# Four interleaved attention layers on one core: a plan that knows the blocks of PE's program, transfers that ScalarE may issue, a second score tile and another division in the last chunk

## The chip, the core and the metric

The kernel runs on one core of a Trainium2 chip. The metric is the time of one execution on the device in microseconds; of each kernel several runs are taken and their median is given. A profiled execution has a time of its own.

The engines are named as the profile names them: PE multiplies matrices (PEld is its loading of weights), DVE is the vector engine, ACT the scalar engine, POOL the general one, SP issues transfers.

## The reference

Four layers in the order A, B, A, B, each `x = x + attention(layernorm(x))`, on x of 2048 x 512 in float32, with 32 heads of 16. Cut to what matters:

```python
def _A_ref(x, wqkv, wo):                 # W, dil = 8, 2
    q, k, v = heads(x @ wqkv)
    idx = pos[:, None] - off[None, :]    # eight keys back, every second one
    logits = where(idx >= 0, einsum("bhsd,bhswd->bhsw", q, kg) * scale, -1e9)
    o = einsum("bhsw,bhswd->bhsd", softmax(logits), vg)
    return merge(o) @ wo

def _B_ref(x, wqkv, wo):                 # W = 256
    scores = q @ k.T * Dh ** -0.5        # the last 256 keys of each query
    p = softmax(where(mask, scores, -1e9))
    return merge(p @ v) @ wo
```

## The kernel before

**Tiling.** The sequence is cut into 8 chunks of 256 rows. Layers 0 and 1 run chunk by chunk (A of chunk c, then B of chunk c), then layers 2 and 3: sixteen pairs A0, B0 to A15, B15. Float32 products of activations and weights are made of three float16 products (high x high, high x low, low x high), which are PE's long part: `proj_t` (L1014) for queries and keys and `proj_n` (L1041) for values and the output.

**A chunk of layer A** (`layer_a`, L1117). Scores of 32 queries against a window of 39 keys are 64 small matmuls for each half of the chunk (L1172). ACT copies them out of the banks into one tile `s` (L1181), transfers put them in memory and fetch the eight wanted ones of each query back (`sd<-s`, `l<-sd`), DVE and ACT make the softmax, the result goes through memory once more (`ptd<-bands`, `ptt<-ptd`), and 128 small matmuls mix the values (L1281).

**A chunk of layer B** (`layer_b`, L1298). Queries and keys are split into high and low float16 parts (L1310, L1313), put in memory and fetched in another arrangement (`re<-eh`, `re<-el` L1323; `stk<-re` L1334). A first pass of scores (L1392) gives each query its maximum: DVE masks (L1411) and reduces (L1407), and the maximum goes through memory into two rows of the queries' tile (`md<-mt` L1443, `stk<-md` L1449). A second pass of scores (L1543) has the maximum subtracted already; ACT takes the exponential (L1553, L1565), POOL or DVE masks it (L1582, L1576), and PE multiplies by the values with a column of ones (L1598), so that row 16 of every 32 is the sum to divide by. ACT copies one half of the result (L1615), DVE adds the other (L1612). In all chunks but the last, transfers gather the sums (`rc<-os` L1661) and the rows (`oc<-os` L1666), a reciprocal is made of a small tile (L1670), spread again (`os<-scr`) and multiplied (L1684). In the last chunk the division is made in place per head (L1628 to L1631): transpose, reciprocal of 8 columns, transpose back, multiply; then the rows leave for `oc` (L1641, half of them issued by ACT). `finish` (L1063) splits `oc` into high and low (L1083, L1085), projects, adds x (L1093) and stores.

**What sets the order.** Nothing is scheduled by hand line by line. Every piece of work is a task of the class `Plan` (`add`, L515) with an engine, a cost, what it reads and writes, and the tiles that it holds. The table `ORDER` at the top gives each task a place in its engine's queue; a negative place sends the task to its other engine (`alt`). `Plan.order` (L542) then walks the queues with the costs and emits all instructions in one sequence, each engine's in the order of its places. The table was found outside the kernel, with these costs. For PE the planner also models a clock that halves when PE did little lately, and a store of instructions that is filled at a fixed rate (`FETCH`, `STORE`). All transfers but the four pairs of L1641 are SP's. `IDLE` filler tasks of three matmuls each (L1724) compute nothing that is read; they keep PE busy.

Of the kernel before, what the change touches and what calls it, by code (L numbers as in the profile page):

```python
# [18 lines left out]
P = 128  # L19
# [417 lines left out]
LAG = {"PE": 0.24, "DVE": 0.13, "ACT": 0.16, "POOL": 0.1, "SP": 0.0}  # L437
RATE = 0.33
SLOW = 0.25
LEAVE = {"Q": 0.13, "C": 0.185, "X": 0.15, "V": 0.17, "R": 0.13, "F": 0.105, "": 0.0}  # L440
AGAIN = {"PE": 0.0, "DVE": 0.11, "ACT": 0.12, "POOL": 0.055, "SP": 0.0}
RECENT, WARM, EDGE = 3.4, 0.31, 0.05
FETCH, STORE = 66.0, 130.0
SLACK = 0.6


class Buf:
# [1316 lines left out]
```

## Time and profile before

| | |
|---|---|
| three runs | 1448.49, 1453.19, 1457.79 us; median 1453.19 |
| profiled execution | 1448.63 us, span of its instructions 1446.9 us |
| mean granted clock of PE | 0.960 |
| busy: PE, DVE, ACT, POOL | 1315.5, 865.6, 827.1, 397.4 us |
| transfers | 195.20 MB at a mean of 135 GB/s |

The rows of the page and of its views read: line, engine, operation, what it writes and reads, the shape, how many; then busy time in us and the mean of one in ns; then the idle time of the engine just before them and who ended it. A row of waits reads: who waited, for whom, us in total, how many times, the longest. A row of the source view gives the shortest, the median and the longest duration in ns. Names ending in q are an engine's sequencer, which issues transfers. "Issue" as releaser means that nothing the profile shows was missing. A row of the windows gives for a stretch the busy time and count of PE, PEld, DVE, ACT and POOL, the granted clock, the share of the transfer engines and their rate.

### The profile page before, as it was taken

What the parts mean: (1) busy time and instruction counts of PE and PEld (TensorE: products, weight loads), DVE (VectorE), ACT (ScalarE), POOL (GpSimd) and SP (SyncE); (2) the same over time, 40 slices, a digit from 0 to 9 for tenths busy, and PEclk for the clock granted to TensorE, in tenths of its full rate; (3) what the DMA queues carried; (4) which work ended last, traced back from release to release, by engine and by line L of the source; (5) the groups of instructions that cost most, each with busy time, mean ns of one, the idle gap of its engine ahead of it and who ended that gap; (6) DMA issues with size and microseconds to landing.
All of it is one profiled execution on the core that took longest, in us unless ns stands there. A gap on an engine that the chain in (4) does not pass through costs nothing. (4 is left out here: it accounts for less than half of the span.)

```text
span 1446.9 us, 64325 instructions
## 1 busy us (share of the span) xinstructions
PE 1315.5 (91%) x28126; PEld 863.0 (60%) x28126; DVE 865.6 (60%) x1967; ACT 827.1 (57%) x1299; POOL 397.4 (27%) x848
## 2 busy tenths in 40 slices
PE   9998999899899989989889898999989898898987
PEld 7765566565575746657456464746657475564643
DVE  5636673753747567375662727566463746748495
ACT  7744666456554746636556473837557455564643
POOL 5131222213323122132133130413133321232441
PEclk9999999999999999999899999999999999999988
DMA  8874445535445364552635546364454635435322
GB/s 271 228 191 123 131 122 142 141 109 141 113 115 153 86 175 113 164 138 92 145 91 163 139 137 153 106 176 98 147 135 122 166 84 160 129 105 146 114 72 61
DMA packets 185234, 195.20 MB, mean 135 GB/s; under 512 B 92892, under 2 KB 123356, under 8 KB 184952
## 3 DMA queue, kind: packets, MB, share of 16 engines
q1 hardware_dynamic: 184696, 190.83, 48.6%
q8 instruction: 220, 3.60, 1.1%
q14 instruction: 62, 0.51, 0.1%
q10 hardware_dynamic: 256, 0.26, 0.1%
HBM read 94.11 MB, written 79.36 MB: 120 GB/s over the span
## 5 line engine op out<-in xcount | busy, mean ns | idle before, releaser
L1407 DVE TENSOR_REDUCE m<-banks 128x2 f32<-128x512 f32 x448 | 301.5, 688 | 8.7
L1553 ACT ACTIVATE p<-banks,sclB 128x896 f32<-128x896 f32 x224 | 220.8, 1007 | 69.6 <-PE banks L1543 65.0
L1411 DVE COPY_PREDICATED banks<-trm,banks 128x128 f32<-128x128 int16 x448 | 123.6, 291 | 147.2 <-PE banks L1392 131.6
L1582 POOL TENSOR_SCALAR_AFFINE_SELECT ps<-ps 64x256 f32<-64x256 f32 x300 | 119.5, 420 | 301.0 <-ACT ps L1565 294.2
L1582 POOL TENSOR_SCALAR_AFFINE_SELECT p<-p 64x256 f32<-64x256 f32 x292 | 116.4, 420 | 218.3 <-ACT p L1553 206.3
L1392 PE MATMUL banks<-stk,stk 48*64 48x128 f16 (+3 forms) x3584 | 140.5, 247 | 38.6 <-DMA stk<-re 12.0
L1392 PEld LDWEIGHTS <-stk 48*64 48x64 f16 x3584 | 81.5, 110 | 115.7 <-issue 89.1
L1543 PE MATMUL banks<-stk,stk 64*64 64x128 f16 (+3 forms) x3584 | 119.3, 240 | 23.4 <-DMA stk<-md 7.2
L1598 PE MATMUL banks<-p,v 64*32 64x192 f32 (+1 forms) x3584 | 122.0, 373 | 13.3 <-issue 8.5
L1565 ACT ACTIVATE ps<-banks,sclB 128x768 f32<-128x768 f32 x112 | 100.5, 901 | 40.6 <-PE banks L1543 33.0
L1543 PEld LDWEIGHTS <-stk 64*64 64x64 f16 x3584 | 70.1, 109 | 76.1 <-issue 61.6
L1313 DVE SCALAR_TENSOR_TENSOR el<-banks,eh 128x512 f16<-128x512 f32 x64 | 42.8, 688 | 101.4 <-ACT eh L1310 57.6
L1181 ACT COPY s<-banks 128x624 f32<-128x624 f32 x64 | 74.3, 1262 | 45.5 <-DMA sd<-s 19.0
L1598 PEld LDWEIGHTS banks<-p,v 64*32 64x32 f32 x3584 | 65.6, 110 | 48.3 <-issue 21.0
L1615 ACT COPY os<-banks 128x256 f32<-128x256 f32 x112 | 41.0, 372 | 85.0 <-PE banks L1598 83.5
L1598 PE MATMUL banks<-ps,v 64*32 64x64 f32 (+1 forms) x3584 | 71.8, 256 | 4.5 <-issue 4.3
L1598 PEld LDWEIGHTS banks<-ps,v 64*32 64x32 f32 x3584 | 66.3, 110 | 11.1 <-issue 8.1
L1026 PE MATMUL banks<-xh,wA0h 128*128 128x256 f16 x256 | 71.1, 278 | 1.4 <-DMA xh<-ht 1.1
L1281 PE MATMUL banks<-ptt,vs 39*32 39x64 f32 x4096 | 58.8, 239 | 14.3 <-DMA ptt<-ptd 7.7
L1027 PE MATMUL banks<-xl,wA0h 128*128 128x256 f16 x256 | 70.8, 276 | 0.4 <-DMA xl<-xn 0.4
L1612 DVE TENSOR_TENSOR os<-os,banks 128x256 f32<-128x256 f32 x104 | 42.1, 415 | 48.4 <-ACT os L1615 40.3
L1028 PE MATMUL banks<-xh,wA0l 128*128 128x256 f16 x256 | 70.9, 277 | 0.0
(217 smaller groups left out, 3070.5 us busy)
## 6 DMA issues: line engine op xcount, KB each, us to landing
stk<-re SPq DMA_DIRECT2D x256, 96.0 KB
sd<-s SPq DMA_DIRECT2D x128, 156.0 KB
re<-eh SPq DMA_DIRECT2D x128, 128.0 KB
ptt<-ptd SPq DMA_DIRECT2D x128, 96.0 KB
vs<-vd SPq DMA_DIRECT2D x64, 156.0 KB
vd<-ve SPq DMA_DIRECT2D x32, 256.0 KB
xm<-y SPq DMA_DIRECT2D x32, 256.0 KB
re<-el SPq DMA_DIRECT2D x64, 128.0 KB
```

The source lines that it names most:

```text
L1026: nc.tensor.matmul(ps[mp].t[:, i], wh, xh, start=k == 0, stop=False)
L1027: nc.tensor.matmul(ps[mp].t[:, i], wh, xl, start=False, stop=False)
L1028: nc.tensor.matmul(ps[mp].t[:, i], wl, xh, start=False, stop=k == 3)
L1181: nc.scalar.copy(S_.t.rearrange("p k (s r) -> p r s k", r=4)[:, 2 * i : 2 * i + 2], pbs[i].t[:, :, 0 : 8 * WIN].rearrange("p r (s k) -> p ...
L1392: nc.tensor.matmul(o, lhs, k, start=True, stop=True, tile_position=(64 * par, 64 * h))
L1407: nc.vector.tensor_reduce(out=m.t[:, :, u, qb], in_=ps.t[:, :, 0 : 2 * P], op=ALU.max, axis=AX.X)
L1411: nc.vector.copy_predicated(t[:, :, 0:64], trm[:, 0].bitcast(I16).unsqueeze(1).broadcast_to([P, 2, 64]), t[:, :, C : C + 64])
L1543: nc.tensor.matmul(ps.t[64 * h : 64 * h + 64, par, at + x0 : at + x0 + q1 - q0], stk[hf, kt][r, col, k0 : k0 + 64], stk[hf, 0][r, col, q0: ...
L1553: nc.scalar.activation(big.t[:, 2 * i : 2 * i + 2], ps.t[:, :, 0:448], AF.Exp, scale=scl["B", 1])
L1565: nc.scalar.activation(small.t.rearrange("p (i m) x -> p m i x", i=2), ps.t[:, :, 0:384].rearrange("p m (i x) -> p m i x", i=2), AF.Exp, s ...
L1582: E.affine_select(out=v, in_=v, pattern=[[0, 4], [a, 64]], compare_op=op, fill=0.0, base=0, channel_multiplier=-a)
L1598: nc.tensor.matmul(acc.t[32 * mm : 32 * mm + 32, h, q0:q1], vv[r, blk, 17 * hd : 17 * hd + 32], x.t[r, mm, x0 : x0 + q1 - q0], start=begin ...
```

## The change

- **Supply.** The store filled at a fixed rate is replaced by a count of PE's instructions: at place 140 of each block of 256 a block is asked for, and place 193 of the next block has to wait until 4.2 us after that. The number of instructions of each task (`rec`) is corrected with it, and so are some costs.
- **ScalarE may issue.** Ten kinds of transfers get `alt=("ACT", ...)`: `shelve`, `band`, `window`, `put`, `get` of layer A; `put`, `stack`, `mput`, `mget`, `gather`, `gather_o`, `spread` of layer B. In the program SP's issues go from 1656 to 1357 and ACT's from 8 to 307. The 60 transposing transfers stay on SP.
- **Two score tiles.** The pool of `s` has two buffers. The room comes from smaller constants: the value tiles share one padding, `maskt` is 256 wide, `nul` one column, `ones` and the padding's source use a buffer of the small exponentials, and the throw-away output of the norms is one byte wide. The first chunk's maxima write their masked scores back to the banks.
- **Last chunk.** After the addition PE spreads row 16 of every 32 over the 32 rows (four matmuls against a column of the identity), and DVE takes the reciprocal of all 256 columns and multiplies. The heads are taken in the order 0, 2, 1, 3 of their quarters, `oc` is split by halves of the features, not of the rows, and the output projection takes its first half of the features as soon as those are there.
- **Orders.** All tables are new, with 122 filler tasks in place of 110.

```diff
-IDLE = 110
+IDLE = 122
-LEAVE = {"Q": 0.13, "C": 0.185, "X": 0.15, "V": 0.17, "R": 0.13, "F": 0.105, "": 0.0}
+LEAVE = {"Q": 0.1, "C": 0.13, "X": 0.18, "V": 0.14, "R": 0.1, "F": 0.095, "": 0.0}
-FETCH, STORE = 66.0, 130.0
-SLACK = 0.6
+SLACK = 0.6, 0.25
+SUPPLY = 4.2
...
-                store = min(STORE, store + FETCH * (now - seen))
-                us = max(us / clock, (t.rec - store) / FETCH)
-                store = min(STORE, store + FETCH * us - t.rec)
-                seen = now + us
+                us /= clock
+                wait = 0.0
+                for x in range(n + 1, n + t.rec + 1):
+                    if x % 256 == 140:
+                        asked, told = told, now + wait + us * (x - n) / t.rec
+                    elif x % 256 == 193 and x > 256:
+                        wait = max(wait, asked + SUPPLY - now - us * (x - n) / t.rec)
+                n += t.rec
+                us += wait
...
-    for name, bufs in (("px", 4), ("pqm", 1), ("pk", 1), ("psc", 1), ...
+    for name, bufs in (("px", 4), ("pqm", 1), ("pk", 1), ("psc", 2), ...
...
+        halves = []
+        if last:
+            for g in range(2):
+                vh, vl = Val(oh), Val(ol)
+                halves.append([vh, vl])
+                sg = slice(2 * g, 2 * g + 2)
+                plan.add("ACT", 0.52, lambda sg=sg: nc.scalar.copy(oh.t[:, sg], o.t[:, sg]), r=vo[g], w=[vh])
+                plan.add("POOL", 1.12, lambda E, sg=sg: E.tensor_tensor(out=ol.t[:, sg], in0=o.t[:, sg], in1=oh.t[:, sg], op=ALU.subtract),
+                         r=[*vo[g], vh], w=[vl], mode="S", alt=("DVE", 0.6))
...
-            proj_n(T, 3, oh, ol, [vh, vl], t, ps, vps)
+            proj_n(T, 3, oh, ol, halves if last else [[vh, vl]] * 2, t, ps, vps)
...
-                    plan.add("SP", 0.64, put, r=ve[n], w=[vre[par][z]], size=128)
+                    plan.add("SP", 0.62, put, r=ve[n], w=[vre[par][z]], size=128, alt=("ACT", 0.68))
-                plan.add("SP", 1.3, stack, r=vre[0] + vre[1], w=[vst[hf, i, hp]], size=192)
+                plan.add("SP", 1.3, stack, r=vre[0] + vre[1], w=[vst[hf, i, hp]], size=192, alt=("ACT", 1.35))
...
-        for j in range(4):
+        for j in (0, 2, 1, 3) if final else range(4):
...
-                                    out=unread[:, x0 : 3 * P], in0=ps.t[:, par, x0 : 3 * P], in1=maskt[:, x0:], scale=1.0, scalar=NEG,
+                                    out=ps.t[:, par, x0 : 3 * P], in0=ps.t[:, par, x0 : 3 * P], in1=maskt[:, x0 - P :], scale=1.0, scalar=NEG,
...
-                def divide(hp=hp, hq=hq, hf=hf, acc=acc, sh=sh, f=both_):
-                    f()
-                    v = sh.t[:, 0:C].rearrange("p (b x) -> p b x", x=32)
-                    r = flat(os_[hf])[:, (2 * hp + hq) * C : (2 * hp + hq + 1) * C]
-                    a = acc.t[:, 0, 0:C]
-                    nc.vector.transpose(sh.t[:, 0:C], a)
-                    nc.vector.reciprocal(v[:, :, 16:17], v[:, :, 16:17])
-                    nc.vector.transpose(r.rearrange("p (b x) -> p b x", x=32), v[:, :, 16:17].broadcast_to([P, 8, 32]))
-                    nc.vector.tensor_mul(r, a, r)
-                plan.add("DVE", 2.0, divide, r=[vacc, vhf], w=[vos[hf][hp], vsh])
+                plan.add("DVE", 0.36, both_, r=[vacc, vhf], w=[vsm])
+                pb = Banks(psum, 1, [P, D])
+                def across(pb=pb, some=some):
+                    for m in range(4):
+                        nc.tensor.matmul(pb.t[32 * m : 32 * m + 32, 0:C], idf[:, 32 * m + 16 : 32 * m + 17].broadcast_to([P, 32]), some(),
+                                         start=True, stop=True, tile_position=(0, 32 * m))
+                def divide(pb=pb, sh=sh, some=some):
+                    nc.vector.reciprocal(sh.t[:, 0:C], pb.t[:, 0:C])
+                    nc.vector.tensor_mul(some(), some(), sh.t[:, 0:C])
+                plan.add("PE", 0.43, across, r=[vsm], w=[vpb], mode="C", act=0.107, rec=16)
+                plan.add("DVE", 0.75, divide, r=[vpb, vsm], w=[vos[hf][hp], vbr])
```

**Transfers of the last B chunk.** SP's queue before, where the rearranged queries and keys are fetched (`stk<-re`), the rows and sums of the chunk before leave (`oc<-os`, `rc<-os`), and the first maxima are put down (`md<-mt`):

```order
L1334 DMA stk_2_131<-re_7_1_25803 48x1x1024 x4
L1334 DMA stk_0_129<-re_7_0_25916 48x1x1024 x2
L1334 DMA stk_0_132<-re_7_0_25916 48x1x1024 x2
L1666 DMA oc_6_25739<-os_6_1_25961 16x1024 x4
L1661 DMA rc_6_25677<-os_6_1_25961 16x1x64 x4
L1334 DMA stk_2_134<-re_7_1_25803 48x1x1024 x2
L1443 DMA md_7_0_26279<-mt_7_0_26271 4x32x32 x2
```

ACT's queue in the changed kernel at the same place, between the last exponentials (`ps_6`) and copies (`os_6`) of the chunk before and the first of this one (`mt_7` is the maximum, `v` the values):

```order
L1589 ACTIVATE ps_6_6_26077<-banks,sclB_172 128x2x2x192
L1358 DMA stk_2_132<-re_7_1_25802 48x1x1024 x2
L1639 COPY os_6_1_25968<-banks 128x256 x2
L1358 DMA stk_0_130<-re_7_0_25917 48x1x1024 x2
L1358 DMA stk_0_127<-re_7_0_25917 48x1x1024 x2
L1694 DMA oc_6_25671<-os_6_1_25968 16x1024 x4
L1454 ACTIVATE mt_7_0_26266<-mr_7_0_26254 128x32
L1368 ACTIVATE v_134<-banks 128x32x16 x2
```

Ten issues that were SP's stand in ACT's queue, ahead of the first maximum of the chunk and of the copy of its values.

**Scores of layer A on PE.** The last A chunk before: one score task (32 matmuls of float32, `k` and `qm`) stands alone between maxima of layer B (`stk`) and projections; its fellow stands 17 rows above.

```order
L1392 LDWEIGHTS stk_0_129
L1392 MATMUL banks<-stk_1_130,stk_0_129 64x256
L1172 MATMUL banks<-k_7_22767,qm_7_23481 64x39 x32
L1046 LDWEIGHTS xl_7_23078
L1046 MATMUL banks<-wA2h,xl_7_23078 128x512
```

The same place in the changed kernel:

```order
L1057 LDWEIGHTS xl_7_23093
L1057 MATMUL banks<-wA2h,xl_7_23093 128x512
L1196 MATMUL banks<-k_7_23130,qm_7_23494 64x39 x64
L1416 LDWEIGHTS stk_0_127
L1416 MATMUL banks<-stk_2_129,stk_0_127 64x128
```

The two tasks follow each other. Such pairs are 17 of the 47 rows of this line before and 30 of 34 now.

**The last two heads on DVE.** Before, each head is added, transposed, inverted, transposed and multiplied in one go:

```order
L1612 TENSOR_TENSOR banks<-os_7_1_27072,banks 128x256
L1628 STREAM_TRANSPOSE sh_27248<-banks 128x256
L1629 RECIPROCAL sh_27248<-sh_27248 128x8
L1630 STREAM_TRANSPOSE os_7_1_27072<-sh_27248 128x256
L1631 TENSOR_TENSOR os_7_1_27072<-banks,os_7_1_27072 128x256
```

Now, for both heads:

```order
L1636 TENSOR_TENSOR os_7_1_27083<-os_7_1_27083,banks 128x256 x2
L1657 RECIPROCAL sh_27277<-banks 128x256
L1658 TENSOR_TENSOR os_7_1_27083<-os_7_1_27083,sh_27277 128x256
L1657 RECIPROCAL sh_27282<-banks 128x256
L1658 TENSOR_TENSOR os_7_1_27083<-os_7_1_27083,sh_27282 128x256
L1087 TENSOR_TENSOR ol_7_27303<-oc_7_26900,oh_7_27301 128x512
```

Both additions stand ahead of both reciprocals, and what follows is the split of one half of the features.

More of the change, by code (lines that the diff above doesn't have):

```diff
@@ L770 @@
     plan.begin("S")
+    plan.add("POOL", 0.3, lambda: nc.gpsimd.memset(ones.t[0:4, 0, 0:P], 1.0), w=[vone])
     plan.add("POOL", 1.8, lambda: nc.gpsimd.memset(ptt, 0.0), w=[vptt])
@@ L1054, in proj_n @@
                 nxt = Val(ps)
-                plan.add("PE", 0.217 if low else 0.433, lambda k=k, low=low: part(k, low), act=0.213 if low else 0.426,
-                         r=[*vals, vwt[T, s], *chain], w=[vps, nxt], mode="F")
+                plan.add("PE", 0.217 if low else 0.433, lambda k=k, low=low: part(k, low), act=0.213 if low else 0.426, rec=2 if low else 4,
+                         r=[*vals[k // 2], vwt[T, s], *chain], w=[vps, nxt], mode="F")
                 chain = [nxt]
@@ L1061, in rows, with finish @@
         return slice(c0 + t, c0 + C, 2) if T == "A" else slice(c0 + t * P, c0 + (t + 1) * P)
-    def finish(l, c, o, vo):
+    def finish(l, c, o, vo, last=False):
         T = layers[l]
@@ L1068, in finish @@
         oh, ol = (buf("poh", [P, 4, C], F16, "o", f"o{z}{l}_{c}") for z in "hl")
+        halves = []
[7 more added lines that the diff above has]
+                         r=[*vo[g], vh], w=[vl], mode="S", alt=("DVE", 0.6))
         for t in range(2):
             ps = Banks(psum, 1, [P, D])
-            vh, vl, vps = Val(oh), Val(ol), Val(ps)
+            vps = Val(ps)
+            if not last:
+                vh, vl = Val(oh), Val(ol)
             sl = slice(t * P, (t + 1) * P)
-            if T == "A":
+            if last:
+                pass
+            elif T == "A":
                 def part(x, sl=sl):
@@ L1247, in layer_a, with window, put, get @@
             vvs = Val(vs)
[L1249 removed]
+            def window(E, t=t, vs=vs):
                 x = vd[l][t]
                 for bb in range(2):
[L1252 removed]
+                    E.dma_start(vs.t[64 * bb : 64 * bb + WIN],
                                       bass.AP(tensor=x.tensor, offset=x.offset + (c * P + 64 * bb) * D, ap=[[D, WIN], [32 * D, 2], [1, D]]))
[L1255 removed]
+            def put(E, t=t):
                 x = ptd[t]
[L1257 removed]
+                E.dma_start(bass.AP(tensor=x.tensor, offset=x.offset, ap=[[130 * H, 64], [64 * H, WIN_], [1, 2 * H]]),
                                   bands[64 * t : 64 * t + 64].rearrange("p k s u -> p k (s u)"))
[L1260 removed]
+            def get(E, t=t):
                 x = ptd[t]
@@ L1350, in layer_b @@
         o = buf("po4", [P, 4, C], F32, "ob", f"oc{l}_{c}")
-        vog = []
+        vog = [[], []] if final else []
         os_ = {}
@@ L1394, in layer_b @@
                     if first:
-                        plan.add("PE", 0.172, scores, r=[vst[hf, 0, hp], vst[hf, now, hp]], w=[vps], mode="R", act=0.14, rec=8)
+                        plan.add("PE", 0.172, scores, r=[vst[hf, 0, hp], vst[hf, now, hp]], w=[vps], mode="R", act=0.14, rec=4)
                     else:
@@ L1448, in mget @@
                     p0 = 64 * par + 48
-                    nc.sync.dma_start(stk[hf, 0][p0 : p0 + 2, 4 * hp : 4 * hp + 4].rearrange("p u t -> p (u t)"), v[par])
+                    E.dma_start(stk[hf, 0][p0 : p0 + 2, 4 * hp : 4 * hp + 4].rearrange("p u t -> p (u t)"), v[par])
             plan.add("DVE", 0.13, mrow, r=vm, w=[vmr])
@@ L1514, in values @@
                                         o = o[:, qo * P : (qo + 1) * P]
-                                    nc.tensor.matmul(o, v[:, jj, 17 * h : 17 * h + 32], rhs, start=z == 0 and (b == 0 or first),
+                                    nc.tensor.matmul(o, v[:, 17 * (H * jj + h) : 17 * (H * jj + h) + 32], rhs, start=z == 0 and (b == 0 or first),
                                                      stop=z == 1 and b == 1, tile_position=(0, 32 * mm), skip_group_check=True)
                         nxt = Val(acc)
-                        plan.add("PE", 0.67, values, r=[vp2, *vvt[(c - 1 + b) % 3], *([chain] if chain else [])], w=[vacc, nxt], mode="C", act=0.16, rec=64)
+                        plan.add("PE", 0.67, values, r=[vp2, *vvt[(c - 1 + b) % 3], *([chain] if chain else [])], w=[vacc, nxt], mode="C", act=0.16, rec=32)
                         chain = nxt
@@ L1611, in both_ @@
                 def both_(acc=acc, some=some):
-                    nc.vector.tensor_tensor(out=acc.t[:, 0, 0:C] if final else some(), in0=some(), in1=acc.t[:, 1, 0:C], op=ALU.add)
+                    nc.vector.tensor_tensor(out=some(), in0=some(), in1=acc.t[:, 1, 0:C], op=ALU.add)
                 vhf = Val(os_[hf])
@@ L1673, in layer_b, with spread @@
         vbc = Val(os_[1])
-        def spread():
-            nc.sync.dma_start(flat(os_[1]), scr.t.unsqueeze(0).broadcast_to([16, 8, 4 * C]))
-        plan.add("SP", 0.55, spread, r=[vscr, *vog], w=[vbc], size=840)
+        def spread(E):
+            E.dma_start(flat(os_[1]), scr.t.unsqueeze(0).broadcast_to([16, 8, 4 * C]))
+        plan.add("SP", 0.55, spread, r=[vscr, *vog], w=[vbc], size=840, alt=("ACT", 0.65))
         vo = [[], []]
@@ L1697 @@
     for some in ((0,), (1, 2)):
-        pad = buf("ps1", [P, 2, 64], F32, "rc", f"pad{some[0]}")
+        pad = buf("pp7", [P, 4, 192], F32, "p7", f"pad{some[0]}")
         vpad = Val(pad)
@@ L1733 @@
             layer_b(l + 1, c)
-    both = {"DVE": nc.vector, "POOL": nc.gpsimd, "ACT": nc.scalar}
+    both = {"DVE": nc.vector, "POOL": nc.gpsimd, "ACT": nc.scalar, "SP": nc.sync}
     for t in plan.order():
```

112 lines of the change are left out of this document (53 added, 59 removed), and 789 rows, old and new, of the table ORDER.

## The prediction

> **What bounds the kernel now.** I read the page first, then what the tensor engine waited for, then the sync engine's issues line by line, and last the end of the span as a timeline.
>
> ```profile
> span 1446.9 us, 64325 instructions
> PE 1315.5 (91%) x28126; PEld 863.0 (60%) x28126; DVE 865.6 (60%) x1967; ACT 827.1 (57%) x1299; POOL 397.4 (27%) x848
> q8 instruction: 220, 3.60, 1.1%
> ```
>
> PE carries work for 1315.5 us and is idle for 1446.9 - 1315.5 = 131.4 us. No other engine is above 60%, so time can come out of this kernel in two ways only: PE waits less, or its busy time runs at a better rate. The third row is a queue that brings instructions: 3.60 MB in 220 packets is 16.4 KB each, and 2 x 28126 = 56252 PE instructions over 220 packets is 256 per packet. So PE's program arrives in blocks of 256. What the 131.4 us were spent on, by the longest rows of PE's own waits:
>
> ```profile
> PE banks L1598 <- issue: 12.8, 6, 4.2
> PE banks L1392 <- DMA stk<-re: 12.0, 14, 1.8
> PE banks L1392 <- DVE m L1407: 9.4, 25, 1.2
> PE banks L1281 <- DMA ptt<-ptd: 7.7, 12, 2.1
> PE banks L1543 <- DMA stk<-md: 7.2, 11, 1.6
> PE banks L1392 <- ACT s L1181: 5.5, 5, 2.9
> PE banks L1281 <- issue: 4.5, 7, 1.0
> PE banks L1543 <- DVE m L1407: 4.5, 13, 1.0
> PE banks L1048 <- ACT oh L1083: 4.4, 1, 4.4
> PE banks L1172 <- issue: 4.3, 5, 1.6
> PE banks L1543 <- issue: 3.5, 3, 1.5
> ```
>
> No single wait leads. "Issue" (nothing that the profile shows was missing) is 12.8 + 4.5 + 4.3 + 3.5 = 25.1 us, transfers 12.0 + 7.7 + 7.2 = 26.9 us, and VectorE and ScalarE share most of the rest. One of the issue stalls, in time:
>
> ```profile
> 644.41 0.85 PE L1598 MATMUL banks<-p,v 64*32 64x256 f32 x14
> 648.45 0.39 PE L1598 MATMUL banks<-p,v 64*32 64x192 f32 x7 [3.19 <-issue]
> ```
>
> It falls in the middle of one run of equal matmuls, whose data had all arrived. Counted along PE's records, sequencer records included, the long gaps of this kind stand at instruction 193 of a block of 256, wherever much fewer than 4.2 us lie between there and instruction 140 of the block before. That is the rule that the changed planner writes down, and the trace bears it out.
>
> **The change part by part.** The profiled execution took 1448.6 us around its span of 1446.9; the sum is made against 1448.6, which stands 4.6 us under the runs' median of 1453.2.
>
> *Supply of instructions.* The new planner charges each such place. I walked both orders with the mean interval that the trace gives each kind of matmul: before, 60 stretches from place 140 to place 193 hold less than 4.2 us of work, 50 us too little in all; in the new order 45 do, 35 us too little. That is 30% off 25.1 us. Nothing to 25.1 us gained; I take **-8**.
>
> *Transfers off the sync engine.* 299 of its 1656 issues move to ScalarE. Prices of an issue, and who was late for it:
>
> ```profile
> L1334 SPq DMA_DIRECT2D stk<-re x256: 536/588/1667, 113.4 to 1387.0; - x128
> L1661 SPq DMA_DIRECT2D rc<-os x120: 502/587/1581, 159.3 to 1383.1; - x120
> 1369.58 7.78 SPq L1334 DMA_DIRECT2D stk<-re x10
> DVE el L1313 <- DMA re<-eh: 27.5, 8, 5.9
> L1641 ACTq DMA_DIRECT2D oc<-os x8: 500/598/878, 1411.9 to 1431.6; - x8
> ```
>
> At 0.588 us each, 1656 issues fill about 970 of 1447 us, and in the last chunk ten follow each other for 7.78 us while PE and VectorE want what they bring. 299 x 0.588 = 176 us leave that queue, 18%. The gain lies between nothing (PE's wait is then the transfer's own flight, not its issue) and 26.9 us. 18% of 26.9 is 5; since the two lines that stand in such trains, stk<-re and re<-eh, give the most of what is moved, and VectorE's 27.5 us behind the same lines delays the maxima that PE waits for, I take twice that, **-10**. The Trainium skill (DMA: Bandwidth & Descriptors, Issuing engines are not separate DMA queues) says that starting transfers from several engines only saves the sequencer's issue time, usually small beside the transfer; here the trace has that issue time at two thirds of the span. By the page alone this term would be near nothing and the sum 10 us later.
>
> *What ScalarE pays.* 299 x 0.598 = 179 us of issuing come on top of its 827.1. Its idle time holds them by the sum (1006 of 1447). But what stands behind an issue that waits for its source stands still too: exponentials, copies out of the banks. PE's waits for ScalarE are 5.5 + 4.4 us in the two rows above; if they and their smaller kin, some 18 us without the score copies, grow as ScalarE's load (1006/827), that is 4; if everything that falls on a busy ScalarE (57% of 179 us) reached PE, 102. The nearest row says the small end; I take **+5**.
>
> *Second score tile.* L1181 copies scores into a tile that a transfer must first have emptied:
>
> ```profile
> ACT s L1181 <- DMA sd<-s: 19.0, 7, 5.2
> ```
>
> With two tiles this wait has no reason left, and the two score tasks of a chunk can follow each other on PE. Of it 5.5 us reached PE in the row above. Nothing to 5.5, if ScalarE is then late with something else or not: **-5**.
>
> *The last chunk.* Rows for the old division and the new one:
>
> ```profile
> L1628 DVE STREAM_TRANSPOSE sh<-banks 128x256 f32<-128x256 f32 x8 | 3.6, 450 | 0.3
> L1629 DVE RECIPROCAL sh<-sh 128x8 f32<-128x8 f32 x8 | 1.6, 206 | 0.3
> L1630 DVE STREAM_TRANSPOSE os<-sh 128x256 f32<-128x256 f32 x8 | 3.6, 446 | 0.3
> L1612 DVE TENSOR_TENSOR banks<-os,banks 128x256 f32<-128x256 f32 x8 | 3.4, 424 | 1.4 <-ACT os L1615 1.4
> L1631 DVE TENSOR_TENSOR os<-banks,os 128x256 f32<-128x256 f32 x8 | 3.4, 424 | 0.3
> L1230 DVE RECIPROCAL mx<-mx 128x64 f32<-128x64 f32 x16 | 8.8, 553 | 0.7
> ```
>
> Old, per head: 424 + 450 + 206 + 446 + 424 = 1950 ns. New: an addition, a reciprocal over 128x256 and a product, 424 + r + 424. From 8 to 64 elements the reciprocal grows by (553 - 206)/56 = 6.2 ns an element, so r = 206 + 248 x 6.2 = 1.74 us, an estimate, and the new chain is 2.59 us, 0.64 more for each of 8 heads; the planner counts 0.75 for r and product together. The Trainium skill (VectorE: DVE Perf Modes, First, the fixed hardware budget) has the reciprocal as an iterative divide repeated 8 times; by that and the page's 0.96 GHz r would be 2.1 us, an estimate, and the end 0.8 us later. The order puts both last additions ahead of both reciprocals, so the last product ends 0.42 + 2 x (1.74 + 0.42) = 4.7 us after the second addition begins, not 2.08 (1428.95 to 1431.03 below): +2.6. Against it stands what follows:
>
> ```profile
> 1428.95 0.42 DVE L1612 TENSOR_TENSOR banks<-os,banks 128x256 f32<-128x256 f32 x1
> 1430.61 0.42 DVE L1631 TENSOR_TENSOR os<-banks,os 128x256 f32<-128x256 f32 x1
> 1434.28 1.14 ACT L1083 CAST oh<-oc 128x512 f16<-128x512 f32 x2 [6.03 <-DMA oc<-os]
> 1434.96 0.61 PE L1048 MATMUL banks<-wB3h,oh 128*128 128x512 f16 x1 [4.44 <-ACT oh L1083]
> 1442.86 0.38 PE L1046 MATMUL banks<-wB3h,ol 128*128 128x512 f16 x1
> ```
>
> All 24 final projections wait for the last landing and take 8.3 us. In the new order half of them need only heads that were divided earlier, and fill the 3.3 us in which PE sat idle for that landing: up to -4.1. Together **-2**, between +3 and -5.
>
> *PE's added work.* 36 more filler matmuls and the 32 that carry the sums across. By the fillers' row, 48.3 us for 330, the 36 cost 5.3 if nothing hides them; they stand where PE would wait: **+2**, of 0 to 8.
>
> *Clock.* A stall can cost twice, where the granted clock falls with it:
>
> ```profile
> L1724 PE MATMUL banks<-idf 128*128 128x256 f16 x330 | 48.3, 289 | 5.1 <-ACT s L1181 1.7 <-POOL idf masks.py:199 1.4 <-DVE y L1093 0.9
> 200.00:250.00 50.00, 45.61 (x1138) 31.77 (x1135) 24.34 (x49) 33.97 (x53) 12.89 (x29) 1.00 0.44 124
> 250.00:300.00 50.00, 42.35 (x904) 24.50 (x904) 31.64 (x66) 19.82 (x31) 11.96 (x27) 0.83 0.55 138
> core 0: 1446.9 us, clock 0.960
> ```
>
> The stretch from 250 holds the longest stall and a clock of 0.83. A mean of 0.960 between full and half is 8% of the span, 116 us, at half, 58 us lost at most. The terms so far shorten PE's idle time by 18 of 131 us, 14%; the same share of 58, mostly on busy time, is 7: **-5**.
>
> The first chunk's maxima now write to the banks rather than to a throw-away tile; L1612 writes os in 415 ns and banks in 424, so 128 of them are some 1 us on an engine that is idle 40%: nothing, or 1 if it were full.
>
> Sum: -8 - 10 + 5 - 5 - 2 + 2 - 5 = -23. From the profiled run that is 1425.6, from the median 1430.2. I forecast the middle, **1428 us**, and 1408 to 1441 for this case alone.
>
> **Rivals.**
> *ScalarE becomes the gate (slower).* Place: the seams between chunks, as in the last one, where the new order has ten issues between the exponentials of one chunk and the first work of the next. Each waiting issue holds the engine, the exponentials behind it hold banks, and PE runs out of banks. 174 groups of issues move. The other terms give -28; for the result to lie above 1468, 1% over the median, ScalarE must cost about 47 us, so from 0.27 us of PE time per moved group it decides; at 0.3 it is 52 and the time is 1448.6 - 28 + 52 = 1473. For it: ScalarE already ends waits of every engine. Against: 43% of it is idle, and a group holds it for 0.6 to 2.4 us. Chance 0.16.
> *The waits only change names (no difference).* The distances along PE from projections to scores and from scores to exponentials are nearly what they were (11 us of PE work each, before and after), so a transfer that is hidden today stays hidden and one that is late stays late. Then supply (-8) is offset by ScalarE and fillers (+7), the rest moves to VectorE's maxima: 1446 to 1452, say 1449. For it: eleven rows and no leader. (The page of the Trainium skill on transfers, named above, would expect this case.) Chance 0.24.
> *Stalls and half clock fall together (larger gain).* Supply -20, transfers -20, score tile -5, clock -12, ScalarE +5: 1397. For it: both come in the same windows. Against: 45 tight stretches remain. Chance 0.10.
>
> **How the numbers follow.** The forecast keeps 0.50. The range runs from 1398, which cuts off half of the large gain, to 1462, beyond which most of the slow case lies. A measurement of this kernel tells about 1% from no change, 14.5 us either way of 1453.2: faster (under 1438.7) has the large gain and all but none of the forecast, 0.60; within 1% 0.24; slower 0.16.
>
> **What would show it.** Right: PE's issue rows near 17 us, its rows on stk<-re, ptt<-ptd and stk<-md under 20 together, no wait of L1205, the score copy, for sd<-s, ScalarE's copies and exponentials late for PE by under 25 us, the granted clock at 0.965 or more, the wide reciprocal between 1.6 and 2.2 us, and 12 projections ahead of the last landing. Wrong: PE rows that end on ScalarE above 50 us, or PE's idle time still 131 us under other names.

## The result and the profile after

The changed kernel takes 1436.87 us, the median of four runs (1434.94 to 1438.52), the kernel before 1454.01 (1448.49 to 1457.79). The ratio is 0.9885, with a 95% interval of 0.985 to 0.9919: 1.2% faster. Forecast were 25 us less, measured are 17. The profiled execution took 1437.16 us around a span of 1435.4, against 1448.63 around 1446.9 before; the two profiles differ by 11.5 us, less than the medians do, since the profile of before was one of that kernel's fastest runs.

The page of the changed kernel, and below it what PE waited for, in the order of the view:

```profile
span 1435.4 us, 64450 instructions
PE 1306.9 (91%) x28226; PEld 861.9 (60%) x28226; DVE 867.4 (60%) x1942; ACT 824.0 (57%) x1298; POOL 392.8 (27%) x841
```

```profile
PE banks L1196 <- issue: 11.6, 8, 2.3
PE banks L1622 <- issue: 10.1, 9, 1.6
PE banks L1416 <- DVE m L1431: 10.0, 25, 0.8
PE banks L1416 <- DMA stk<-re: 8.2, 6, 2.6
PE banks L1305 <- DMA ptt<-ptd: 6.8, 7, 1.8
PE banks L1416 <- issue: 6.5, 6, 2.8
PE banks L1305 <- ACT v L1368: 5.5, 1, 5.5
PE banks L1305 <- issue: 5.1, 3, 2.6
PE banks L1567 <- DMA stk<-md: 3.7, 6, 1.4
...
PE banks L1567 <- issue: 2.3, 3, 1.2
```

PE is idle for 1435.4 - 1306.9 = 128.5 us, 2.9 less than before, but what it waits for has changed. With all rows of the view added up by what ended the wait:

| PE's waits, us | before | after |
|---|---|---|
| transfers | 31.9 | 21.0 |
| ScalarE, the score copy alone | 8.9 | 1.9 |
| ScalarE, all else | 18.3 | 25.5 |
| VectorE | 33.4 | 30.5 |
| issue | 26.5 | 39.5 |

By this view transfers, score copies and VectorE gave back 20.8 us, and the supply of instructions, which the new plan was to mind, and ScalarE's other work took 20.2. So the idle time hardly shrank, and the gain stands in busy time: 1315.5 - 1306.9 = 8.6 us less, although 100 matmuls were added. The reason is in how the page is made. A matmul's end is modelled, some 0.25 to 0.4 us after its start, while the next may start within 20 ns; a wait shorter than that leaves no idle time. So I took the times from one PE instruction's start to the next, and from each the usual one for the same two instructions (the lower quartile over both traces):

| PE, start to start, us | before | after |
|---|---|---|
| the usual times | 897.8 | 895.5 |
| beyond them, with a wait that something ended | 140.8 | 109.0 |
| beyond them, nothing missing, over 0.45 us | 31.0 | 52.7 |
| beyond them, nothing missing, shorter | 377.1 | 377.8 |
| sum | 1446.7 | 1435.0 |

That is the change in one table: 32 us fewer waits, and 22 us more of stops without a visible cause. Split by who ended the wait, a count of the same kind, which finds 35 us in all, has transfers fall from 48.5 to 29.5 us, VectorE from 58.6 to 51.3, the score copy from 9.1 to 2.7 and ScalarE's other work from 30.1 to 29.7. The granted clock stayed, 0.958 against 0.960.

**How a fetch goes.** The issue waits of PE can be followed into queue q8, whose packets the trace holds. Place 140 of one block (places count from 0) and the stop at place 193 of the next, for one of the longest stalls of each kernel, in us:

| | place 140 passes | packet starts | packet ends | PE at 192 | PE goes on |
|---|---|---|---|---|---|
| before | 641.22 | 645.83 | 647.12 | 644.94 | 648.45 |
| after | 1139.52 | 1142.86 | 1144.14 | 1142.38 | 1145.44 |

The second of them in PE's records, between score matmuls of one line:

```profile
1142.37 0.24 PE L1416 MATMUL banks<-stk,stk 48*64 48x128 f16 x4
1145.44 0.70 PE L1416 MATMUL banks<-stk,stk 48*64 48x192 f16 x12 [2.82 <-issue]
```

PE goes on 1.3 to 1.5 us after the packet has ended, in most stalls of both kernels (25% to 75% of them: 1.35 to 1.49 before, 1.30 to 1.49 after). The packet takes 1.1 us (0.9 to 1.6). What varies is the time until it starts. With each packet set against place 140 of its own block, it is 2.02 us in the middle of the changed kernel's 221, 4.75 at 95%, and over 5 in six cases; before it was 1.96 and 4.35, and once 7.2. (Set against the next packet to start, as the expectations below have it, it comes out at 1.8 and 4.3; but in 13 blocks that is still the packet of the block before.) So a fetch, up to PE's next instruction, takes about 4.6 us in the middle, before and after, and two thirds of them take longer than the 4.2 with which the plan counts. Stops of over 0.25 us at place 193 itself number 32 with 36.0 us in the profile of before, and 37 with 50.0 after; "stops" below are these.

### The profile page after: what moved, and what is told of

The parts are those of the page before. It is cut to its first block, busy times and chain, and to the rows that moved or that the text cites. A ratio compares the mean times of both kernels' runs of the same rounds, so it can differ in the third digit from the quotient of the medians.

```text
span 1435.4 us, 64450 instructions
## 1 busy us (share of the span) xinstructions
PE 1306.9 (91%) x28226; PEld 861.9 (60%) x28226; DVE 867.4 (60%) x1942; ACT 824.0 (57%) x1298; POOL 392.8 (27%) x841
## 4 chain that ended last, share of the span: by engine, by line
PE 65%; DMA 12%; DVE 7%; issue 5%; ACT 4%; SPq 4%; ACTq 2%; POOL 1%; DVEq 0%; POOLq 0%
PE banks L1037 7%; PE banks L1622 7%; PE banks L1038 7%; PE banks L1039 6%; PE banks L1059 6%; PE banks L1057 6%; PE banks L1060 5%; PE banks L1567 4%; PE banks L1416 4%; PE banks L1305 3%; PE banks L1196 3%; DVE m L1431 2%; PE banks L1752 2%; DMA stk<-re 2%; DMA re<-eh 1%
## 5 line engine op out<-in xcount | busy, mean ns | idle before, releaser
L1606 POOL TENSOR_SCALAR_AFFINE_SELECT ps<-ps 64x256 f32<-64x256 f32 x280 | 109.7, 414 | 260.4 <-ACT ps L1589 219.0
L1416 PE MATMUL banks<-stk,stk 48*64 48x256 f16 (+3 forms) x3584 | 139.2, 246 | 36.3 <-DVE m L1431 10.0
L1622 PE MATMUL banks<-p,v 64*32 64x192 f32 (+1 forms) x3584 | 114.8, 360 | 5.7 <-issue 1.6
L1205 ACT COPY s<-banks 128x624 f32<-128x624 f32 x64 | 75.1, 1263 | 44.9 <-PE banks L1196 39.5
L1636 DVE TENSOR_TENSOR os<-os,banks 128x256 f32<-128x256 f32 x112 | 45.8, 416 | 69.0 <-ACT os L1639 65.9
L1037 PE MATMUL banks<-xh,wA1h 128*128 128x256 f16 x256 | 71.2, 278 | 0.4 <-DMA xh<-ht 0.2
```

Of the source, the lines that this page charges most:

```text
L1037: nc.tensor.matmul(ps[mp].t[:, i], wh, xh, start=k == 0, stop=False)
L1416: nc.tensor.matmul(o, lhs, k, start=True, stop=True, tile_position=(64 * par, 64 * h))
L1606: E.affine_select(out=v, in_=v, pattern=[[0, 4], [a, 64]], compare_op=op, fill=0.0, base=0, channel_multiplier=-a)
L1622: nc.tensor.matmul(acc.t[32 * mm : 32 * mm + 32, h, q0:q1], vv[r, 17 * (H * blk + hd) : 17 * (H * blk + hd) + 32], x.t[r, mm, x0 : x0 + q1 ...
```

## The experiments

Twelve runs; all but the last were timed beside the kernel before on the same chip. Ratios are to the kernel before; where the comparison wanted is with the changed kernel, its ratio of 0.9885 stands for it, and the interval joins both half-widths as the root of the sum of their squares.

**1. All transfers from SP, in the new orders.** One line of the loop that emits the tasks:

```diff
-        t.fn(both[t.eng]) if t.alt else t.fn()
+        e = "SP" if t.size else t.eng
+        t.fn(both[e]) if t.alt else t.fn()
```

> The changed kernel with all its transfers issued by SP again; the orders of the other engines, banks and buffers stay. Theory 1 (relief of SP's queue is what shortened PE's waits for transfers, 43.7 us before and 26.8 now by our count of PE's gaps): those waits return, and with them 10 to 17 us less ScalarE's share of some 5: 1443 to 1452. Theory 2 (the new orders did it, the issuing engine does not matter): 1437 within 4. Theory 3 (ScalarE pays more for issuing than SP's relief brings): under 1433.

Measured 1495.61 us, ratio 1.0286 (1.0226 to 1.0345), 4.1% over the changed kernel: 59 us, far beyond every theory. PE's waits for transfers lead the view now:

```profile
PE banks L1305 <- DMA ptt<-ptd: 30.3, 22, 5.2
PE banks L1416 <- DMA stk<-re: 21.4, 15, 4.2
PE banks L1416 <- DVE m L1431: 12.3, 23, 3.5
PE banks L1567 <- DMA stk<-md: 11.5, 6, 3.4
```

In all they are 80.2 us, 59 more than the 21.0 of the changed kernel, so they carry the whole difference. And SP itself, in the view of the queue's waits, stands behind sources that are not ready, with the steps of other work behind it:

```profile
SPq L1473 <- DMA md<-mt: 45.2, 32, 5.1
SPq L1467 <- DVE mt L1459: 42.8, 16, 10.4
```

(These two are 33.9 and 37.8 us in the changed kernel, so they have grown by 16 us between them.)

The direction is that of theory 1. The size says more: the new orders are so made that they need two issuers.

**2. The same transfers from ScalarE, in the old orders.**

```diff
     for t in plan.order():
+        who[0] = nc.scalar if t.k in MOVED.get(t.scope, ()) and t.size else nc.sync
         t.fn(both[t.eng]) if t.alt else t.fn()
```

(`who[0]` issues in place of `nc.sync`; `MOVED` lists the 177 groups; the prediction had counted 174.)

> The kernel before, with its own orders, in which the 177 groups of transfers that the change gives to ScalarE are issued by ScalarE at the same point of the program. Theory 1 (SP's queue was the limit): 5 to 12 us faster than before, 1442 to 1449. Theory 2 (orders): 1454 within 4. Theory 3 (a waiting issue holds ScalarE, whose order was not made for it): slower by 5 or more, 1459 and up, with more PE waits that end on ScalarE.

Measured 1451.02 us, ratio 0.9979 (0.9948 to 1.0009): no difference that can be told, so theories 1 and 3 fail as stated. But theory 2 has no ground either, since the waits moved. PE's waits for transfers fell from 31.9 to 7.7 us, a good deal lower than in the changed kernel, and its waits for ScalarE rose from 27.2 to 47.9. The longest rows for ScalarE:

```profile
PE banks L1547 <- ACT p L1557: 6.4, 9, 3.6
...
PE banks L1396 <- ACT ve L1247: 5.5, 4, 3.3
...
PE banks L1396 <- ACT v L1348: 4.5, 3, 4.1
```

So both rivals of this part were right in part: PE's waits for transfers go down by 24 us when the queue is relieved, and its waits for ScalarE go up by 21. (The profiled run took 1459.62 us, 8.6 above the median, so the 21 may be on the high side; that it is the waiting issues that hold ScalarE is read from experiment 2's rows, not tried by itself.) Experiments 1 and 2 together say where the gain sits: neither in the move nor in the orders alone, but in orders made for the move.

**3. One score tile.**

```diff
-("psc", 2)
+("psc", 1)
-S_ = buf("psc", [P, WIN, H], F32, "s", f"s{l}_{c}_{t}")
+S_ = buf("psc", [P, WIN, H], F32, "s", f"s{l}_{c}_{t}", cap=2)
```

(The plan still counts two tiles, so all orders stay; in memory there is one.)

> The changed kernel with one score tile in memory instead of two, everything else alike. Theory 1 (the second tile carries the paired score tasks): the second copy of each of 32 pairs has to wait for the first tile's transfer, about 5 us each by the wait for sd<-s before, and ScalarE and the banks wait with it: 1447 to 1490. Theory 2 (the wait lies beside other work, as 13.5 of its 19.0 us did before): 1437 to 1443.

Measured 1454.71 us, ratio 0.9999 (0.9963 to 1.0036), which is 1.2% (0.7 to 1.7) over the changed kernel. ScalarE's wait for the tile, then PE's for the copies:

```profile
ACT s L1205 <- DMA sd<-s: 41.2, 8, 8.6
```

```profile
PE banks L1416 <- ACT s L1205: 9.4, 7, 3.1
...
PE banks L1622 <- ACT s L1205: 5.4, 4, 3.2
...
PE banks L1752 <- ACT s L1205: 4.0, 2, 3.3
```

Theory 1 holds: the wait for `sd<-s` is back at twice what it was before the change (19.0), and PE's waits for the copies, all rows together, are 19.7 us instead of 1.9. The profiled run took 1445.37 us, 9.3 under the median, so its waits account for some 8 of the 17 us only. In orders with paired score tasks, taking the second tile away loses about all that the change gained; since experiments 1 and 5 lose more than that, such losses can't be added up to shares of the gain.

**4. Blocks moved by 96 instructions.**

```diff
+    for _ in range(48):
+        nc.tensor.matmul(psum[:, 7, 0:1], idf.bitcast(F16)[:, 0:P], idf.bitcast(F16)[:, 0:1], start=True, stop=True)
     for t in plan.order():
```

> The changed kernel with 48 one-column matmuls (96 instructions) at the start of PE's program, so that each block of 256 instructions begins 96 instructions earlier in the work; the matmuls themselves lie in the idle start. Theory 1 (PE stops where a block passes faster than its fetch, whose duration spreads around 4.4 us): with the measured spread of fetches and the measured times between the places, stalls should grow by 27 us by that model, 15 to 27 on the clock: 1452 to 1464, with the stalls again at place 193 of the shifted blocks. Theory 2 (stalls come where the work is dense, whatever the place of the block): 1437 within 4.

Measured 1462.0 us, ratio 1.0051 (1.0014 to 1.0087), 1.7% (1.2 to 2.2) over the changed kernel: 24 us, of which the 48 matmuls are 2.2 (the first projection begins at 19.06 instead of 16.87). They did not hide in the start, against what was expected. The waits:

```profile
PE banks L1622 <- issue: 24.3, 15, 3.2
PE banks L1416 <- DMA stk<-re: 13.3, 10, 3.5
PE banks L1305 <- DMA ptt<-ptd: 9.8, 11, 3.5
PE banks L1196 <- issue: 9.6, 9, 1.9
```

Stops near place 193 rise from 50.0 to 66.3 us (50.0 to 53.6 in the four profiles of the unshifted order, experiments 8, 9 and 10 among them). Theory 1 holds: where the blocks begin matters, though nothing in the work itself has moved.

**5. Queries and keys from SP, the rest of the moved transfers from ScalarE.**

```diff
+        e = "SP" if t.size in (128, 192) else t.eng
+        t.fn(both[e]) if t.alt else t.fn()
```

> The changed kernel with the 132 issues on ScalarE that carry layer B's queries and keys (re<-eh, re<-el and stk<-re) given back to SP, the other 167 left on ScalarE. Theory 1 (these two steps stand in trains on SP's queue and carry most of what sending all back cost, 59 us): 1467 to 1487. Theory 2 (every issue weighs alike: 44% of 59 is 26): 1459 to 1466. Theory 3 (the small steps of maxima, sums and windows are what block SP's queue, since they wait there for late sources): 1437 to 1447.

Measured 1485.65 us, ratio 1.0193 (1.0145 to 1.0242), 3.1% over the changed kernel: about 45 of the 59 us of experiment 1, for 132 of 299 issues. PE waits 32.0 us for `stk<-re` in all (8.5 in the changed kernel). Theory 1 holds: these are the issues that stand in trains.

```profile
PE banks L1416 <- DMA stk<-re: 21.8, 20, 3.8
...
PE banks L1567 <- DMA stk<-md: 9.9, 9, 2.6
...
PE banks L1305 <- DMA stk<-re: 6.5, 1, 6.5
```

**6. The kernel before with its blocks moved.** The edit of experiment 4 in the kernel before.

> The kernel before with the same 48 one-column matmuls (96 instructions) at the start of PE's program. They cost 2.2 us at the start of the changed kernel. Theory 1 (fetches that spread around 4.4 us against the time between the places, whatever the plan): the model that gave 27 us for the changed kernel, where 22 were measured, gives 11 here: 1461 to 1466. Theory 2 (the old plan did not know the blocks, so no place of theirs is better than another): 1454 to 1458.

Measured 1453.92 us, ratio 0.9988 (0.9958 to 1.0019): theory 2, and no trace even of the 2.2 us. The model was right on the stops, which rise from 36.0 to 47.3 us, and wrong on the time: PE's waits for ScalarE and transfers did not grow with them as they did in the changed kernel. That the old plan leaves slack behind the stops is the likely reason; it was not tried.

**7. One-column matmuls that move the blocks.**

```diff
+PADS = {1192: 3, 1215: 1, 1217: 1, 1223: 1, 1342: 2, 1359: 1, 1379: 3, 1380: 6, 1470: 24, 1536: 1, 1543: 6,
...
+    def more(to):
+        for _ in range(pads[0]):
+            nc.tensor.matmul(to, idf.bitcast(F16)[:, 0:P], idf.bitcast(F16)[:, 0:1], start=True, stop=True)
...
+            if kk[0] == 0:
+                more(ps[mp].t[:, i, 0:1])
...
     for t in plan.order():
+        pads[0] = PADS.get(place, 0) if t.eng == "PE" else 0
+        place += t.eng == "PE"
```

(They write a column that the next matmul of the same bank overwrites.)

> The changed kernel with 152 one-column matmuls (304 instructions, 13.5 ns each by the shifted run) in front of 33 of its projections and fillers, so placed by a search over the measured times of the changed kernel that fewer blocks of PE's program pass faster than their fetch. Nothing else moves. Theory 1 (in the changed kernel the blocks lie elsewhere than the plan counts them, since its count runs up to 105 instructions behind PE's records at the end, and that can be mended): the model has 63 us of stalls now and 48 then, 4 us of pads: 11 us less, 1423 to 1431. Theory 2 (stalls follow the chance of each fetch, not the place): 4 us more for the pads, 1439 to 1444.

Measured 1431.69 us, ratio 0.9857 (0.9808 to 0.9905), 0.3% under the changed kernel with an interval of 0.6: not settled by itself; experiment 11 repeats it. The stops fall to 38.4 us. What led here was a count: the planner adds up `rec`, the instructions of each task, and its sum stands 20 too high after the first 100 us against PE's records, is level near 330, and 105 too low at the end (56543 for the whole program, where the trace has 56652 records, 200 of them the sequencer's). So the blocks lie elsewhere than the plan put them.

**8. The old division in the new plan.**

```diff
-                def across(pb=pb, some=some):
...
+                def across():
+                    pass
...
-                    nc.vector.reciprocal(sh.t[:, 0:C], pb.t[:, 0:C])
-                    nc.vector.tensor_mul(some(), some(), sh.t[:, 0:C])
+                    v = sh.t[:, 0:C].rearrange("p (b x) -> p b x", x=32)
+                    nc.vector.transpose(sh.t[:, 0:C], some())
+                    nc.vector.reciprocal(v[:, :, 16:17], v[:, :, 16:17])
+                    nc.vector.transpose(pb.t[:, 0:C].rearrange("p (b x) -> p b x", x=32), v[:, :, 16:17].broadcast_to([P, 8, 32]))
+                    nc.vector.tensor_mul(some(), some(), pb.t[:, 0:C])
```

(PE's 32 spreading matmuls are left out with it.)

> The changed kernel with the division of before in the last chunk: VectorE transposes, inverts 8 columns, transposes back and multiplies, and PE's 32 spreading matmuls are left out; the order of the additions, transfers and projections stays as changed. Theory 1 (the wide reciprocal, 1.75 us of a new 2.6 us chain, is longer than the old chain of 1.95): the two last heads end 1.3 to 1.9 us earlier after the second addition than the 4.95 us now, and the run is 1 to 2 us shorter, 1433 to 1437. Theory 2 (the transfers behind it hide the difference): 1437 within 1.5, with the last landing at the same distance.

Measured 1438.87 us, ratio 0.9897 (0.9865 to 0.9928): over a whole run the difference is too small to see. Over the end it isn't. VectorE's groups in the changed kernel, and in this one:

```profile
L1657 DVE RECIPROCAL sh<-banks 128x256 f32<-128x256 f32 x8 | 14.0, 1753 | 0.6 <-PE banks L1653 0.5
L1658 DVE TENSOR_TENSOR os<-os,sh 128x256 f32<-128x256 f32 x8 | 3.7, 457 | 0.3
```

```profile
L1657 DVE RECIPROCAL sh<-sh 128x8 f32<-128x8 f32 x8 | 1.7, 207 | 0.3
```

From the start of the second of the last two additions (1416.84) to the end of the last product (1421.80) it is 4.96 us in the changed kernel, and 3.59 here (1415.29 to 1418.88): 1.37 us for the new division, as theory 1 has it.

**9. The changed kernel again.** No edit.

> The changed kernel once more, unaltered, beside the next two on the same chip, for a ratio to them: 1437 within 4 by every theory, and the same waits in its profile (issue near 40 us on PE, transfers near 19).

Measured 1437.41 us, ratio 0.9894 (0.9854 to 0.9934). Its runs lie between 1435.10 and 1448.85, and the profiled one has a span of 1447.1, with 53.6 us of stops and, by the view, 27.6 us of waits for transfers instead of 21.0: so much do the same orders differ from run to run. The expected waits of one profile were too narrow.

**10. The first half is split before the last issues.**

```diff
+    tasks = plan.order()
+    early = [tasks.pop(7663), tasks.pop(7663)]
+    early[1].eng = "POOL"
+    tasks[7647:7647] = early
-    for t in plan.order():
+    for t in tasks:
```

> The changed kernel in which ScalarE makes the high part of the last chunk's first half ahead of its last four transfers instead of behind them, and POOL, idle then, the low part in place of VectorE. Theory 1 (this half was ready, and its cast stood behind an issue that waited 6.78 us for the last division): the first projections of that half begin about 1422 minus the start of the second last addition instead of 1424, the PE clock stays full, and the end comes 1 to 3 us earlier: 1434 to 1436 in time, and under 17.5 us from the second addition's start to the end, where it is 18.56. Theory 2 (PE could not have begun before the last landing, since its banks wait for the divisions): 18.3 to 18.8 us and no change.

Measured 1438.11 us, ratio 0.9873 (0.9842 to 0.9905); over the run nothing can be told from experiment 9. In the end it can. The changed kernel, then this one, in time:

```profile
1416.45 6.78 ACTq L1669 DMA_DIRECT2D oc<-os  x4
...
1416.84 0.42 DVE L1636 TENSOR_TENSOR os<-os,banks 128x256 f32<-128x256 f32 x1 [0.37 <-ACT os L1639]
...
1421.37 0.43 DVE L1658 TENSOR_TENSOR os<-os,sh 128x256 f32<-128x256 f32 x1
...
1423.40 0.62 ACT L1086 CAST oh<-oc 128x512 f16<-128x512 f32 x1 [6.59 <-issue]
1424.07 0.39 PE L1059 MATMUL banks<-wB3h,oh 128*128 128x512 f16 x1 [2.19 <-ACT oh L1086]
```

```profile
1423.57 0.42 DVE L1636 TENSOR_TENSOR os<-os,banks 128x256 f32<-128x256 f32 x1 [0.37 <-ACT os L1639]
...
1426.55 0.62 ACT L1086 CAST oh<-oc 128x512 f16<-128x512 f32 x1 [3.02 <-PE banks L1060]
1426.56 3.61 ACTq L1669 DMA_DIRECT2D oc<-os  x4
1427.31 1.16 POOL L1087 TENSOR_TENSOR ol<-oc,oh 128x512 f16<-128x512 f32 x1 [7.88 <-ACT oh L1086]
...
1428.44 0.38 PE L1059 MATMUL banks<-wB3h,oh 128*128 128x512 f16 x1
```

In the changed kernel the cast of the half that was ready stands behind ScalarE's own issues, which wait 6.78 us for the last division. Ahead of them, PE begins 4.87 us after the second addition instead of 7.23, and from that addition to the end of the span it is 15.87 us instead of 18.60 (1439.44 - 1423.57, and 1435.44 - 1416.84). Theory 1 holds: 2.7 us. Part of it is PE's pace: in the changed kernel the granted clock is 0.81 from 1422 to 1426 and 0.77 in the 4 us after that, and projections follow each other by some 0.43 us at first; here it is 1.00 from 1424 to 1436, and they follow by 0.21.

**11. Pads and early split together.** Both edits.

> The padded kernel (152 one-column matmuls) with the early split of the last chunk's first half together: the one gives 4 us less by its median with an interval that reaches no gain, the other 1 to 3. If both hold: 1429 to 1432, ratio to the kernel before 0.981 to 0.986. If the pads' 4 us were chance: 1435 to 1437.

Measured 1431.65 us, ratio 0.9837 (0.9802 to 0.9873), beside 0.9894 of experiment 9 on the same chip: 0.6% less, 0.0 to 1.1. The stops are at 40.0 us, and the end takes 15.90 us from the second addition. It has the lowest median of the study, 1.6% under the kernel before, though experiment 7 stands right beside it (1431.69); that it beats the changed one is likely, not settled.

**12. More load.**

```diff
+    room = [far.tile([512, 512], F32, name=f"room{i}") for i in range(8)]
-    for t in plan.order():
+    for n, t in enumerate(plan.order()):
+        if n % 80 == 40 and n > 800:
+            nc.sync.dma_start(room[n // 80 % 8], a_wqkv[:, 0:512])
```

> The changed kernel with some 85 further transfers of 1 MB from memory to memory, spread over the run on SP's queue, read by nobody: 44% more bytes. Only the fetches of PE's program are looked at. Theory 1 (a fetch waits behind packets of data): the time from place 140 to the start of the fetch's packet, 1.8 us in the middle and 4.3 at 95% now, grows to 2.3 and over 5, and the packet itself takes longer than 1.07. Theory 2 (its spread has nothing to do with the load of the transfers): within 0.15 and 0.4 of what it is.

The 86 transfers are 46% more bytes, and the one run of this kernel took 1599.24 us at a granted clock of 0.908. The fetch's packet starts 2.80 us after place 140 in the middle and 6.21 at 95% (2.02 and 4.75 in the changed kernel, 2.20 and 4.73 in experiment 9), so theory 1 holds for the wait. It fails for the packet, which takes 1.05 us as before. Stops rise to 74.0 us. What in the load delays one fetch and not the next is open: within a run, the bytes in flight at the request and the delay hardly go together (correlations of 0.13 to 0.19 in the four profiles tried).

## Why the prediction was right, and where it was not

The time and its direction were right (1436.87 in 1398 to 1462, forecast 1428). That the sum came within 9 us is in part luck: the supply went 21 us the other way, and what made up for it are waits shorter than the view can show, of transfers (19 us less by the starts) and of VectorE (7 us less), for which the sum had no term.

One profile's waits are also not exact. In the profiles of the changed kernel and of experiments 8, 9 and 10, whose orders differ from it at the end alone, transfers make 18.6 to 27.6 us, ScalarE's work without the score copies 20.6 to 30.0, and issue 39.5 to 41.8. So of the figures below, which are of the changed kernel's profile by the view, the one for the supply is firm and the next two are not. Term by term:

- **Supply, -8: wrong, +13.** The step that failed is the walk by mean intervals against a fixed 4.2 us, and that the stalls would shrink with what it found. In the traces, the time from place 140 to the record just ahead of place 193 of the next block is under 4.2 us in 30 blocks before and in 20 after (the walk had 60 and 45). So tight stretches are fewer by a third, but what they lack in all is not less: 19.3 us before, 21.2 after. The rest is in the fetches, which take 3.7 to 6.6 us (10% to 90%; 3.8 to 6.3 before). Where less than 4.6 us of time lie between the places, a fetch takes 4.4 us in the mean before, and 4.6 to 4.8 in the changed kernel and experiments 8, 9 and 10. Why it is longer there is open; experiment 1, with PE's same order and nearly the same stretches (19, lacking 19.9 us), has only 38.5 us of stops, so the order alone does not make it. "The trace bears it out" was said of the place, which is right, and taken for the duration, which is not one number. Experiments 4 and 7 show that the place of the blocks decides between 38 and 66 us of stops in the new orders (36 tight stretches that lack 41.8 us, and 13 that lack 11.1); experiment 6 that in the old ones this did not show in the time.
- **Transfers, -10: right by this profile, -10.9** (31.9 to 21.0; the three rows named come to 18.7, forecast were under 20; -4.3 by the profile of experiment 9, and -19 by the starts). The reason given, trains of issues of queries and keys, is what experiment 5 shows. But the sum treated it as a price of the move; experiment 2 shows that the move alone takes 24 us off PE's waits for transfers and nothing off the time. The Trainium skill (DMA: Bandwidth & Descriptors, Issuing engines are not separate DMA queues), by which this term was near nothing, agrees with experiment 2 and not with experiments 1 and 5, where the issuing engine alone makes 59 and 45 us.
- **What ScalarE pays, +5: near, +7 by the view** (18.3 to 25.5 without the score copies; forecast were under 25 for copies and exponentials), and nothing by the starts (30.1 to 29.7), so the size is not settled. One place makes most of the 7, and it is the slow rival's mechanism, not at the seam that the rival named but at 1128 us:

```profile
1115.65 0.57 ACTq L1276 DMA_DIRECT2D vs<-vd  x1
...
1118.54 4.17 ACTq L1467 DMA_DIRECT2D md<-mt  x2
...
1122.75 3.10 ACTq L1694 DMA_DIRECT2D oc<-os  x4
...
1126.89 0.71 ACTq L1473 DMA_DIRECT2D stk<-md  x2
...
1127.65 0.60 ACT L1368 ACTIVATE v<-banks 128x512 f32<-128x512 f32 x1 [12.12 <-DMA stk<-md]
...
1128.30 2.01 PE L1305 MATMUL banks<-ptt,vs 39*32 39x64 f32 x121 [5.52 <-ACT v L1368]
```

Four groups of issues, of which the later ones wait for their sources, hold ScalarE for 12 us; the copy of the values stands behind them, and PE for 5.5 us. A stop of 4.5 to 5.8 us ahead of the same mixing matmuls stands in the profiles of experiments 3, 4 and 7 to 11; in that of experiment 1, where SP issues all, it is missing. At the seam of the last chunk, where ten issues were feared, ScalarE had 8.11 us before its next work and waited for VectorE; they cost nothing.
- **Score tile, -5: right in sign, too small.** The row itself fell by 7.0 (8.9 to 1.9), and the copy no longer waits for `sd<-s`. Without the tile the new orders lose 17 us (experiment 3). Read from the old row, a tile's worth is what it costs in the old orders; the pairs of score tasks that it allows were counted and not priced.
- **Last chunk, -2: wrong, +0.6.** From the start of the second of the last two additions to the end it is 18.60 us (17.97 before: 1428.95 to 1446.92). The division was sized well (r 1.75 us, forecast 1.74, and not the 2.1 of the other estimate; 4.96 us to the last product, forecast 4.7). The step that failed is that half of the final projections fill the wait for the last landing: only two of the 24 began ahead of it (at 1424.07 and 1424.30; ScalarE's cast of the other half, which waits for that landing, began at 1424.81), since ScalarE's first cast stood behind ScalarE's issues (experiment 10). The prediction did not ask what stands behind those issues.
- **PE's added work, +2: open; clock, -5: wrong, 0.** The fillers and spreading matmuls are 53.4 - 48.3 = 5.1 and 5.4 us more busy time; what of it is on the path cannot be told. The granted clock did not rise (0.958, 0.960): idle time had not shrunk by 18 us but by 2.9, so there was little for it to follow.

Of the rivals, "the waits only change names" describes two thirds of what happened (22 of 32 us), with the supply as the new name, and experiment 2 as a whole. The large gain was to come from supply and transfers falling together; they did not.

## What to carry to other kernels

In this kernel a queue that is busy two thirds of the time was worth relieving only together with an order that is made for the second issuer: count what stands behind each issue that waits, on the engine that takes it over, the casts of the last stage too. A new buffer should be priced by the order that it allows, not by the wait that it ends. And where a plan rests on a count of instructions or on a measured latency, hold both against the trace once more after the change, with the spread of the latency and not its middle.

## What the hardware showed unexpectedly

The time between PE's request for a block of its program and the start of the packet varies from 0.8 to over 7 us in one run (a middle of 2.0), and grows with the load of the transfers (2.8 with 46% more bytes, in one run), while the packet (1.1 us; 0.9 to 1.5 from 10% to 90%) and the 1.3 to 1.5 us from its end to PE's next instruction vary far less. A one-column matmul of 128 rows costs PE 27 ns with its weight load (48 of them from 1.41 to 2.72 us in experiment 4), so it is a cheap way to move a block's place. And the same program differs by 14 us between runs (1435 to 1449).
